# Thresholded attention with an ELU layer: scores that begin 64 columns further in their PSUM banks, and eight score products in another order

## The chip, the cores and the metric

The kernel runs on one core of one Trainium2 chip. The metric is device time in microseconds (us) of one execution; before the change the median of three runs is 1311.3 us (1310.9 to 1311.52).

## What is computed

Two blocks follow each other. For each of 8 sequences and 8 heads, with 576 tokens and 64 numbers per head, in float32:

```python
scores = (1/8) * q @ k.T                                  # 576 x 576 for each head
scores = where(scores >= max(scores) - tau, scores, -1e9)
attn   = exp(scores - max(scores)); attn /= sum(attn) + 1e-9
x      = attn @ v                                         # heads side by side: 4608 x 512
h      = x @ w_in                                         # 512 -> 2048
out    = where(h > 0, h, exp(min(h, 0)) - 1) @ w_out      # 2048 -> 512
```

## The kernel before

**Tiling.** Heads are handled in 32 pairs. The head dimension of 64 fills half of the 128 rows of TensorE, so that head 0 of a pair lies on rows 0 to 63 and head 1 on rows 64 to 127 (`r = slice(h * D, (h + 1) * D)`): products of the two heads use different halves of the array. The 576 queries of a pair are four tiles of 128 (`i` = 0 to 3) and a rest of 64 for both heads together (`i` = 4). P is 128, S 576, D 64, T 32, TAIL 64.

**The stage that matters here.** The first nine pairs run another scheme. From pair 9 on (`JOINED`), a loop over the pairs `pr` issues for each: `tail_step` (the scores of the 64 last queries, L672; the products with v of the pair two before, L677 and L685), then for `half` = 0 and 1 a `wide_step` (L1501), each followed by 14 quarters of the feed-forward block (L1238 is the product with w_in, L1378 that with w_out). There are 23 such pairs, and so 46 wide steps. Pairs alternate between two kinds of feed-forward work: after some, both halves are followed by L1238, after others by L1378.

**A wide step.** `wide_scores` computes scores of two query tiles (`s` = 0, 1) and two heads (`h` = 0, 1), four blocks of 128 x 576 numbers, into one PSUM tile of 128 x 2560, which is five banks of 512 columns. Block (h, s) begins at column (2h + (s xor h)) x 576, so that the order in the tile is (0,0), (0,1), (1,1), (1,0), and the last 256 columns are unused. A product must not cross a bank, so each block is cut in two where a bank ends: eight products, issued in an order written out by hand (L620). Each names the head `h`, the tile `s`, the first key column `c` and the number of columns `n`; its stationary operand is 128 queries of `qT`, its moving operand `n` keys of `kT`, and it appears twice in the profile, as two passes. After the eight products comes, on VectorE, a maximum of each block (L632), on GpSimd the bound (L638), on ScalarE the exponential (L642), and on VectorE the mask (L646).

**What waits for what.** `on_banks` (L586) makes dependencies by bank: a product waits for the ScalarE and VectorE instructions that touched its bank since the last product there, and a reader waits for all products into the banks it reads. In the product loop there is also a one-column ScalarE copy into `seen` (L628), which reads block (1,1) in bank 2 after its first piece: through it the last product of the step, also in bank 2, waits for that piece. In `tail_step` the products with v use banks 1 and 2 and are copied out by ScalarE (L695, L701); the tail's scores use banks 3 and 4 and are read by VectorE and ScalarE.

**Order.** Instructions of each engine run in the order in which they are issued. That order is fixed when the program is made: `on_pe` advances a planned TensorE clock by a planned cost (2.15 us for `wide_scores`), and `at` puts the other engines' work on an agenda by planned times, shifted by a table of corrections. The planned costs are numbers in the code, not measurements of a run.

Of the kernel before, what the change touches and what calls it, by code (L numbers as in the profile page):

```python
# [137 lines left out]
def kernel(  # L138
# [13 lines left out]
    B, H, S, D = q.shape  # L152
# [5 lines left out]
    T = 32  # L158
# [427 lines left out]
    def on_banks(made, ap):  # L586

        ins, needed, starts = made.ins, [], [ap.offset % (5 * 512)]
        for step, n in ap.ap[1:-1]:
            starts = [s + step * k for s in starts for k in range(n)]  # L590
        engine = str(ins.engine)
        for x in sorted({b for s in starts for b in range(s // 512, (s + ap.ap[-1][1] - 1) // 512 + 1)}):
            others = [i for e, i in accesses.setdefault(x, []) if e != engine]
            needed += others
            if others and engine == str(nc.tensor.engine):
                accesses[x] = []
            accesses[x].append((engine, ins))
        for other in needed:
            tc.add_manual_dep(ins, other.name,
                              mybir.DependencyInfo(mybir.DependencyClass.Sync, mybir.DependencyReason.DATA), reason="bank")  # L600
        for e in (nc.tensor, nc.scalar, nc.vector):
            if str(e.engine) != engine:
                tc.declare_no_dep(ins, group=str(e.engine), keep=needed, reason="other banks")
        tc.add_to_no_dep_group(engine, ins)

    def open_step(pr, i, w):
        st = open_steps[pr, i] = vectors(pr)
        st["w"] = w
        return st

    def wide_scores(pr, half):

        qT, kT, _ = pairs[pr]
        for s in range(2):
            i = 2 * half + s
            st = open_step(pr, i, turned_by[1 - s])
            for h in range(2):
                c = (2 * h + (s ^ h)) * S
                st["sc", h], st["e", h] = wide[0][:, c : c + S], st["w"][:, h * S : (h + 1) * S]
        for h, s, c, n in ((0, 0, 0, 512), (1, 1, 0, 384), (0, 0, 512, 64), (1, 1, 384, 192),  # L620
                           (1, 0, 0, 320), (0, 1, 0, 448), (1, 0, 320, 256), (0, 1, 448, 128)):
            i, r = 2 * half + s, slice(h * D, (h + 1) * D)
            k0 = c + (0 if h else TAIL)
            o = open_steps[pr, i]["sc", h][:, c : c + n]
            on_banks(nc.tensor.matmul(o, qT[r, i * P : (i + 1) * P], kT[r, k0 : k0 + n], start=True, stop=True,  # L625
                                      skip_group_check=True), o)
            if n == 384:
                on_banks(nc.scalar.copy(seen, o[:, :1]), o[:, :1])  # L628

    def wide_max(pr, i, h):  # L630
# [545 lines left out]
    with tc.manual_schedule():  # L1176
# [324 lines left out]
        def wide_step(pr, half):  # L1501
            t = clock[0]
            on_pe(2.15, lambda: wide_scores(pr, half))
            e = t + 2.15
            for s in range(2):
                i = 2 * half + s
                at(e + 1.55 + 1.5 * s, lambda i=i: wide_bounds(pr, i), f"bound{i}")
                for h in range(2):
                    k = 2 * s + (h ^ s)
                    at(e + 0.75 * k, lambda i=i, h=h: wide_max(pr, i, h), f"max{i}{h}")  # L1510
                    at(e + (1.6, 3.0, 4.7, 5.6)[k], lambda i=i, h=h: wide_exp(pr, i, h), f"exp{i}{h}")
                    at(e + (3.0, 4.3, 6.5, 6.9)[k], lambda i=i, h=h: wide_mask(pr, i, h), f"mask{i}{h}")
                finish_of(pr, i, e + (5.1, 7.8)[s], e + (8.4, 10.5)[s])
            if pr + 1 < NP:
                at(e + 5.2, lambda: (prep_k if half else prep_q)(pr + 1), f"prep{half}")
                if not half:
                    at(e + 6.1, lambda: scale_q(pr + 1), "qscale")
                if half:
                    at(e + 6.1, lambda: copy_k(pr + 1), "kcopy")
                    if pr + 2 < NP:  # L1520
                        at(e + 6.1, lambda: load(pr + 2, ("qm",), True), "loadq")
                elif pr > JOINED:
                    at(e + 6.1, lambda: load(pr + 1, ("km",), True), "loadk")
            extras(e + 0.3, e + 1.2, e + 4.2, e + 10.4, e + 12.0)
# [126 lines left out]
```

## Time and profile before

The profiled execution took 1310.99 us, of which the span of the core is 1309.2 us.

| what | value |
|---|---|
| median of three runs | 1311.3 us |
| profiled execution, its span | 1310.99 us, 1309.2 us |
| TensorE (PE) busy | 1294.1 us, 99% of the span |
| VectorE (DVE) busy | 1016.5 us, 78% |
| GpSimd (POOL) busy | 802.8 us, 61% |
| ScalarE (ACT) busy | 559.6 us, 43% |
| granted TensorE clock, mean of the span | 1.0 |
| first and last score product of a wide step (L625) | 292.1 us, 1062.0 us |

A profile row such as "PE f L1238 MATMUL" names the engine, the tile that is written, the line and the operation. PEld stands for loads of the stationary operand. In a row the shape "64*128 64x512" means 64 rows by 128 columns of the array, and 512 columns streamed on 64 partitions. Passes on TensorE are pipelined, so the recorded durations of neighbouring passes overlap, and what a pass occupies is the distance from its start to the next start. Idle time of an engine that does not set the end costs nothing.

### The profile page before, as it was taken

The numbers are of one execution on the slowest core, as the hardware profiler recorded it, in microseconds if no ns is written. First come the engines' busy times: TensorE is split into PE (matmuls) and PEld (weight loads), VectorE is DVE, ScalarE is ACT, GpSimd is POOL, SyncE is SP. The second block draws the span as 40 slices with busy tenths as digits, with TensorE's granted clock in tenths as the row PEclk, the third lists the DMA queues.
The fourth block names the chain that finished last, engine by engine and source line by source line (L and its number), as shares of the span: only waits on it lengthen the run. The fifth ranks groups of instructions, "written<-read, shape, count | busy, mean of one in ns | idle before, by whom it ended". The sixth has DMA issues, their size and how long they took to land.

```text
span 1309.2 us, 21968 instructions
## 1 busy us (share of the span) xinstructions
PE 1294.1 (99%) x6971; PEld 1007.7 (77%) x6971; DVE 1016.5 (78%) x2199; ACT 559.6 (43%) x1216; POOL 802.8 (61%) x1186
## 2 busy tenths in 40 slices
PE   9999999999999999999999999999999999999998
PEld 7667656556788887777777787777777888888887
DVE  6878886879888988898889979897989882545534
ACT  5677763225252535344444434352525260421320
POOL 4667875777466765766576747574858473624533
PEclk9999999999999999999999999999999999999999
DMA  6344655987888988898979888989899875221211
GB/s 138 77 106 125 177 111 140 258 229 219 222 233 237 258 227 251 220 268 209 245 211 264 231 234 225 258 235 240 229 253 256 221 215 173 92 73 60 93 61 33
DMA packets 323379, 248.94 MB, mean 190 GB/s; under 512 B 208832, under 2 KB 285120, under 8 KB 323264
## 3 DMA queue, kind: packets, MB, share of 16 engines
q1 hardware_dynamic: 321328, 247.06, 69.2%
q8 instruction: 55, 0.90, 0.3%
q10 hardware_dynamic: 1936, 0.48, 0.2%
q14 instruction: 60, 0.49, 0.1%
HBM read 162.40 MB, written 85.07 MB: 189 GB/s over the span
## 4 chain that ended last, share of the span: by engine, by line
PE 92%; DVE 4%; DMA 1%; issue 1%; POOL 1%; SPq 1%; ACT 0%; DVEq 0%; POOLq 0%; ACTq 0%
PE f L1378 29%; PE f L1238 29%; PE sc L625 8%; PE sc L685 7%; PE f L776 4%; PE rt L438 3%; PE sc L367 3%; PE f L736 3%; PE pv L578 2%; PE sc L677 1%; PE sc L672 1%; PE pv L573 1%; DVE w L428 1%; DMA there<-x 0%; POOL w L401 0%
## 5 line engine op out<-in xcount | busy, mean ns | idle before, releaser
L401 POOL TENSOR_SCALAR w<-w,rs 128x576 f32<-128x576 f32 x196 | 164.8, 848 | 80.7 <-DVE rs L435 65.5
L632 DVE TENSOR_REDUCE mx<-sc 128x1 f32<-128x576 f32 x207 | 148.2, 749 | 35.7 <-PE sc L625 33.0
L642 ACT ACTIVATE w<-sc,mx 128x576 f32<-128x576 f32 x115 | 83.0, 740 | 114.4 <-DVE mx L632 96.8
L1238 PE MATMUL f<-xt,sw 128*128 128x256 f32 x512 | 123.8, 384 | 0.8 <-ACT xt L695 0.5
L1238 PE MATMUL f<-xt,w_in_sb 128*128 128x256 f32 x512 | 122.4, 381 | 0.3 <-ACT w L1252 0.3
L638 POOL TENSOR_SCALAR th<-mx,ntau 128x2 f32<-128x2 f32 (+1 forms) x115 | 34.3, 298 | 141.2 <-DVE mx L632 141.2
L512 DVE STREAM_TRANSPOSE x<-w 128x512 f32<-128x512 f32 (+2 forms) x146 | 98.1, 706 | 13.5 <-POOL w L401 12.9
L1238 PEld LDWEIGHTS f<-xt,w_in_sb 128*128 128x128 f32 x512 | 96.1, 190 | 16.1 <-ACT w L1252 3.3
L1238 PEld LDWEIGHTS f<-xt,sw 128*128 128x128 f32 x512 | 93.7, 190 | 18.2 <-ACT xt L695 0.9
L625 PE MATMUL sc<-kT,qT 64*128 64x512 f32 (+4 forms) x736 | 107.5, 423 | 0.0
L1238 PE MATMUL f<-x,w_in_sb 128*128 128x256 f32 x448 | 106.1, 379 | 1.3 <-ACT g L1299 1.3
L625 PEld LDWEIGHTS sc<-kT,qT 64*128 64x128 f32 x736 | 80.8, 186 | 34.2 <-issue 16.8
L1378 PE MATMUL f<-w_out_sb,g 128*128 128x256 f32 x448 | 107.1, 382 | 0.0
L1378 PE MATMUL f<-w_out_sb,s 128*128 128x256 f32 x448 | 107.0, 382 | 0.0
L1378 PE MATMUL f<-t,s 128*128 128x256 f32 x448 | 105.8, 379 | 0.0
L1325 POOL TENSOR_TENSOR s<-g 128x256 f32<-128x256 f32 x104 | 80.3, 778 | 29.4 <-PE f L1378 20.1
L646 DVE SCALAR_TENSOR_TENSOR w<-sc,th,w 128x576 f32<-128x576 f32 x115 | 89.7, 810 | 10.3 <-ACT w L642 10.1
L1238 PEld LDWEIGHTS f<-x,w_in_sb 128*128 128x128 f32 x448 | 85.0, 190 | 13.3 <-ACT g L1299 1.7
L1378 PEld LDWEIGHTS f<-w_out_sb,g 128*128 128x128 f32 x448 | 84.1, 190 | 12.9 <-issue 0.7
L1378 PEld LDWEIGHTS f<-t,s 128*128 128x128 f32 x448 | 85.1, 190 | 11.6
L1378 PEld LDWEIGHTS f<-w_out_sb,s 128*128 128x128 f32 x448 | 84.2, 190 | 12.3
L401 POOL TENSOR_SCALAR e<-e,rs 128x576 f32<-128x576 f32 x92 | 68.5, 748 | 35.8 <-DVE rs L435 34.5
(189 smaller groups left out, 2853.7 us busy)
## 6 DMA issues: line engine op xcount, KB each, us to landing
there<-x SPq DMA_DIRECT2D x412, 144.0 KB, 3.5
wTb<-there SPq DMA_DIRECT2D x53, 576.0 KB, 6.3
wTa<-there SPq DMA_DIRECT2D x50, 576.0 KB, 5.0
sw<-win_sums SPq DMA_DIRECT2D x62, 384.0 KB, 4.3
t<-wout_sums SPq DMA_DIRECT2D x45, 512.0 KB, 5.4
qm<-in_q_dram SPq DMA_DIRECT2D x124, 72.0 KB, 4.5
vm<-in_v_dram SPq DMA_DIRECT2D x64, 128.0 KB, 3.4
wst<-in_moe_w_in_dram SPq DMA_DIRECT2D x16, 512.0 KB, 4.0
```

The costliest lines, as they stand in the source:

```text
L367: nc.tensor.matmul(scs[h][:, a, :HALF], qs[r], kT[r, k0 : k0 + HALF], start=True, stop=True)
L401: nc.gpsimd.tensor_scalar(wv, wv, st["rs"][:, h : h + 1], 1.0, ALU.mult, ALU.mult)
L512: nc.vector.transpose(x[:, :, c0 : c0 + nc_], src.rearrange("p (c g n) -> p g c n", c=nc_, n=T))
L625: on_banks(nc.tensor.matmul(o, qT[r, i * P : (i + 1) * P], kT[r, k0 : k0 + n], start=True, stop=True, skip_group_check=True), o)
L632: on_banks(nc.vector.tensor_reduce(st["mx"][:, h : h + 1], st["sc", h], axis=AX.XY if i == NC else AX.X, op=ALU.max, negate=True), st["sc" ...
L642: on_banks(nc.scalar.activation(st["e", h], st["sc", h], AF.Exp, bias=st["mx"][:, h : h + 1]), st["sc", h])
L646: on_banks(nc.vector.scalar_tensor_tensor(st["e", h], st["sc", h], st["th"][:, h : h + 1], st["e", h], ALU.is_ge, ALU.mult, accum_out=st[" ...
L685: on_banks(nc.tensor.matmul(o, vm[:, h, c], parts[part][:, g0:g1, h * (NC + 1) + c], start=False, stop=(c == NC - 1), skip_group_check=Tru ...
L776: nc.tensor.matmul(cur[c, i][:, :DM], hidden(c, ft % NU, 1)[:, 0, ft // NU, i], w_out_sb[:, ft], start=(ft == 0), stop=(ft == NFT - 1))
L1238: nc.tensor.matmul(loc["banks"][place], left[:, j], right[:, j], start=(begins and j == 0), stop=(j == 1), skip_group_check=True)
L1325: engine.tensor_tensor(o, x, y, op)
L1378: nc.tensor.matmul(place(m), lhs, rhs, start=(begins and v == 0), stop=(v == RU - 1), skip_group_check=True)
```

## The change

Every block of a wide step begins 64 columns (2 x T) further in the five banks. The bank ends therefore cut the blocks elsewhere: 448 + 128, 384 + 192, 320 + 256 and 256 + 320 columns instead of 512 + 64, 448 + 128, 384 + 192 and 320 + 256. No product has 64 columns any more. The eight products are issued in another order, and the condition that places the `seen` copy names the first piece of block (1,1) directly. Each block still lies in the same two banks as before.

```diff
             for h in range(2):
-                c = (2 * h + (s ^ h)) * S
+                c = 2 * T + (2 * h + (s ^ h)) * S
                 st["sc", h], st["e", h] = wide[0][:, c : c + S], st["w"][:, h * S : (h + 1) * S]
-        for h, s, c, n in ((0, 0, 0, 512), (1, 1, 0, 384), (0, 0, 512, 64), (1, 1, 384, 192),
-                           (1, 0, 0, 320), (0, 1, 0, 448), (1, 0, 320, 256), (0, 1, 448, 128)):
+        for h, s, c, n in ((0, 0, 0, 448), (1, 1, 0, 320), (1, 1, 320, 256), (0, 0, 448, 128),
+                           (1, 0, 0, 256), (0, 1, 0, 384), (1, 0, 256, 320), (0, 1, 384, 192)):
...
-            if n == 384:
+            if (h, s, c) == (1, 1, 0):
                 on_banks(nc.scalar.copy(seen, o[:, :1]), o[:, :1])
```

The order of instructions on VectorE, ScalarE, GpSimd and SyncE is the same in both programs; on TensorE only these eight products differ.

## The prediction

> **What bounds the kernel now.** I read the page first, then the busy time by stretch, because the change touches only the score products at L625, which run from 292 to 1062 us.
>
> ```profile
> span 1309.2 us, 21968 instructions
> PE 1294.1 (99%) x6971; PEld 1007.7 (77%) x6971; DVE 1016.5 (78%) x2199; ACT 559.6 (43%) x1216; POOL 802.8 (61%) x1186
> PE 92%; DVE 4%; DMA 1%; issue 1%; POOL 1%; SPq 1%; ACT 0%; DVEq 0%; POOLq 0%; ACTq 0%
> ```
>
> ```profile
> 292.00:340.00 48.00, 45.99 (x227) 35.49 (x226) 41.71 (x94) 23.25 (x51) 36.02 (x54) 1.00 0.78 207
> 340.00:1062.00 722.00, 722.00 (x4049) 576.50 (x4048) 625.84 (x1380) 309.37 (x682) 464.81 (x697) 1.00 0.88 238
> ```
>
> The columns are the stretch, its length, and busy time of PE, PEld, DVE, ACT and POOL. From 340 to 1062 us PE is busy for all of 722 us at the full granted clock, and the chain of waits for that stretch consists of PE lines alone. DVE is busy for 625.84 / 722 = 87%. So PE time taken out of a wide step should move the end, as long as the others can follow.
>
> Busy says nothing of stalls between passes, so I read the score products by shape.
>
> ```profile
> L625 PE MATMUL sc<-kT,qT 64*128 64x512 f32 x92 | 51.6, 641 | 0.0
> L625 PE MATMUL sc<-kT,qT 64*128 64x448 f32 x92 | 44.6, 565 | 0.0
> L625 PE MATMUL sc<-kT,qT 64*128 64x384 f32 x92 | 41.8, 534 | 0.0
> L625 PE MATMUL sc<-kT,qT 64*128 64x320 f32 x92 | 32.1, 429 | 0.0
> L625 PE MATMUL sc<-kT,qT 64*128 64x256 f32 x92 | 27.2, 376 | 0.0
> L625 PE MATMUL sc<-kT,qT 64*128 64x192 f32 x92 | 22.3, 323 | 0.0
> L625 PE MATMUL sc<-kT,qT 64*128 64x128 f32 x92 | 17.5, 270 | 0.0
> L625 PE MATMUL sc<-kT,qT 64*128 64x64 f32 x92 | 15.2, 245 | 0.0
> ```
>
> The last two fields are the union of busy time and the mean of one pass in ns. The last view is a stretch of PE in order of time: start, length, count.
>
> ```profile
> 713.73 1.89 PE L1238 MATMUL f<-xt,w_in_sb 128*128 128x256 f32 x8
> 715.46 1.89 PE L1238 MATMUL f<-x,w_in_sb 128*128 128x256 f32 x8
> 717.27 2.32 PE L625 MATMUL sc<-kT,qT 64*128 64x512 f32 x16
> 719.52 1.99 PE L1238 MATMUL f<-xt,sw 128*128 128x256 f32 x8
> ```
>
> A wide step occupies PE from 717.27 to 719.52, 2.25 us; 45 of the 46 take this time, and one (324.90 to 327.96) takes 3.06.
>
> **Where the 2.25 us go.** In the rows by shape, 128, 192, 256 and 320 columns lie on a line: (429 - 270) / 192 = 0.83 ns a column, plus 164 ns in which the end of a pass runs on beside the next. Eight passes of 256 columns take 715.46 - 713.73 = 1.73 us, 216 ns each, so a start costs some 3 ns above the columns. By the line, 512 and 384 columns should show 589 and 483 ns; they show 641 and 534, 52 and 51 more. These are the first pieces of the two halves of the array: on the first of two passes a weight load of about 104 ns lies open. The 64 columns should show 217 and show 245; the 448, which follow them in the same half, should show 536 and show 565. That is 2 x 28 + 2 x 29 = 114 ns. I read it so: a pass of 64 columns streams for 53 ns, the load for the pass behind it takes 104, and about 51 of each load lie open, twice. The 192, 256, 320 and 128 show nothing.
>
> The halves run beside each other. Each streams 1152 columns in two passes: 2 x 1152 x 0.83 = 1.91 us, 8 starts x 3 ns = 0.02, the first load 0.10: 2.04. The half of head 0 adds the 0.114: 2.15. The change-over to the next kind of product is 717.27 - 715.46 - 1.73 = 0.08. Sum 2.23 against 2.25 measured. So the half of head 0, with its 64 columns, ends the step, and the half of head 1 is done 0.1 us before it (in the trace its last pass starts 1.84 us into the step and streams 0.21; that of head 0 starts at 2.05 and streams 0.11).
>
> **The change part by part.**
>
> Removed: the 64 columns with their 0.114 us. Added: 128 columns in the middle of head 0's half. A pass of 128 streams for 106 ns against a load of 104, and the last product of before (128 columns) shows 270 ns, on the line; but there only its own second load is seen, and not one of a product behind it. I take 0.009 us for it, between 0 and 0.02. Both halves still stream 1152 columns. Gain per step 0.114 - 0.009 = 0.105 us; from 45 steps 4.7 us. In the long step the half of head 1 is held by a ScalarE copy until 0.95 us and ends last; nothing is gained or lost there.
>
> The queue order costs nothing if a piece's load is only held by the pieces ahead of it and by its own half. The trace shows that the halves pass each other:
>
> ```profile
> L625 PE MATMUL sc<-kT,qT 64*128 64x512 f32 x1 | 0.6, 589 | 0.0
> L625 PE MATMUL sc<-kT,qT 64*128 64x192 f32 x2 | 0.5, 322 | 0.0
> ```
>
> These are the passes in flight from 737.98 to 738.01 us: both passes of the fourth piece (192) and none of the third (64), which stands ahead of it but waits behind the 512 columns of its own half. By this, in the new order the pieces of head 1 start at 0, 0.65, 1.08 and 1.51 us, those of head 0 at 0, 0.86, 1.08 and 1.72, none late.
>
> Here a rule of the Trainium skill differs, "TensorE: Matmul & The Clock Gate", Part 3, The mechanism: matmuls start and end strictly in program order, and weight loads overlap running matmuls only when the row group differs. By the first half of it the old order would run as 1280 columns and the new one as 1152, and the gain would be 128 x 2 x 0.83 ns x 45 = 9.6 us; the rows just shown contradict it for this kernel. The second half speaks against the change, since pieces two and three now share a half; a row named with the rivals contradicts it too.
>
> The waits. Third in the queue is now a piece in bank 3; in first halves it waits for the mask of the tail scores (L646), which by the trace ends 1.39 us before the step in pairs of one kind and 0.25 us after its start in the others. Its load is due at about 0.54 (start 0.65 less a load), so 0.25 us of cover; if the mask came later than that, every 0.1 us would cost as much in 11 steps, and everything behind it on PE would wait too. The 128 columns in bank 1 wait for the copy L695, which ends 0.49 us into the step, and are due at 0.75. The `seen` copy now starts at 1.20 and ends at 1.36; it waits for both first pieces, of which the longer one shrinks from 512 to 448 columns, so I put it at 1.10 to 1.26; the last product's load is due at 1.39. All three cost nothing. The first maximum waits for the sixth product, which ends at 2.10 us; it should end at 1.88, so DVE may begin 0.2 us earlier where it is idle. Nothing on PE in this stage waits for that maximum directly.
>
> What gives some back:
>
> ```profile
> PEld sc L625 <- ACT xt L695: 5.1, 21, 0.2
> PEld f L1238 <- ACT w L1252: 2.3, 10, 0.3
> ```
>
> These are loads that waited between 340 and 1063 us (total, times, longest). The first is the copy just named and is covered. The second comes once in two pairs, 11 us after a second half: ScalarE stands behind DVE work which is busy from before the step, and some 0.1 us of each wait reaches PE. If PE comes 0.105 us earlier and that chain does not, 10 x 0.105 = 1.05 us are lost; if the chain moves along, nothing. I take the middle, 0.5. No other wait on PE is left in that stretch; what becomes late next is this one.
>
> Sum: 4.7 - 0.5 = 4.2 us. The profiled execution's 1310.99 becomes 1306.8; the median of the runs lies 0.3 above it, so 1311.3 becomes 1307.1.
>
> **The rivals.**
>
> No change that can be told (a measurement of this kernel can tell about 0.2%, 2.6 us): the open loads belong to the place in the queue and not to the 64 columns, so that the new 128 columns in the middle cost as much; or DVE, busy for 87%, keeps the pace and PE waits for what it saved. Against the first: 51 open of 104 is just what 53 ns of streaming leave. Against the second: PE waits for DVE's work only in those 10 places. Time 1309 to 1311.3.
>
> Slower: pieces two and three share a half, and the loads of both passes of the second one lie open, 2 x 104 = 0.208 us a step on the half that then ends last. Net 0.208 - 0.105 = 0.103 x 45 = 4.6 us, 1315.9. It decides from about 0.1 us open per step. Against it: in the old order 192 and 320 of head 1 are neighbours too, and the 320 show 429 ns, on the line. For it: only that no neighbours stood so early in the step.
>
> **How the numbers follow.** Forecast 0.83, no change 0.11, slower 0.06. The forecast's own range goes from 1305.4 (4.7 gained, and the ten waits of 0.1 gone as DVE starts earlier, with 0.2 for the scatter of the runs) to 1308.7, the bound of 0.2%. To leave out no more than 2 in 10, the range goes on through most of the no-change case, to 1310.6.
>
> **What would show it.** In the changed profile a wide step should last 2.14 to 2.15 us from its first pass to the next line. The row of 448 columns should lie some 52 ns above the line, that of 320 some 26 (one of its two pieces stands first in its half), and 128, 192, 256 and 384 on it. PE should still be busy through the stage, and the span of the 46 steps shorter by 4 to 5 us. The prediction is wrong if the 128 or the 384 show 25 ns or more above the line (the load stays open), if 256 does (the neighbours), if PE shows new waits for L646 at L625, or if L1252 holds PE for over 0.2 us each time.

## The result and the profile after

The changed kernel takes 1307.2 us in the median of 7 runs (1306.34 to 1307.65) against 1311.52 us for the kernel before, run beside it. The ratio is 0.9965, with a 95% interval of 0.9956 to 0.9974: 3.4 to 5.8 us less. The profiled execution has a span of 1305.3 us, 3.9 less than before.

The page of the changed kernel, first line, busy time of the engines and the chain that ended last:

```profile
span 1305.3 us, 21968 instructions
PE 1289.7 (99%) x6971; PEld 1008.4 (77%) x6971; DVE 1015.5 (78%) x2199; ACT 559.7 (43%) x1216; POOL 802.5 (61%) x1186
PE 92%; DVE 4%; issue 1%; POOL 1%; DMA 1%; ACT 1%; SPq 1%; DVEq 0%; POOLq 0%; ACTq 0%
```

TensorE lost 4.4 us of busy time; the other engines did the same work. Busy time by stretch, with the columns as in the prediction:

```profile
340.00:1058.00 718.00, 717.63 (x4049) 576.98 (x4049) 625.03 (x1381) 309.35 (x682) 464.61 (x697) 1.00 0.88 240
```

The stretch ends where the last score product starts, at 1058.1 us instead of 1062.0, and PE is still busy through it, but for 0.37 us. The score products by shape (union of busy time, mean ns of a pass):

```profile
L625 PE MATMUL sc<-kT,qT 64*128 64x320 f32 x184 | 69.0, 455 | 0.0
L625 PE MATMUL sc<-kT,qT 64*128 64x256 f32 x184 | 47.1, 376 | 0.0
L625 PE MATMUL sc<-kT,qT 64*128 64x448 f32 x92 | 46.7, 588 | 0.0
L625 PE MATMUL sc<-kT,qT 64*128 64x384 f32 x92 | 37.1, 484 | 0.0
L625 PE MATMUL sc<-kT,qT 64*128 64x192 f32 x92 | 22.3, 323 | 0.0
L625 PE MATMUL sc<-kT,qT 64*128 64x128 f32 x92 | 17.6, 272 | 0.0
```

The line through the rows of before (164 ns + 0.83 ns a column) gives 270, 323, 376, 483, 430 and 536 for 128, 192, 256, 384, 320 and 448 columns. Only 448 (52 above) and 320 (25 above, half of its passes) are off it: the first pieces of the two halves. The stretch that answers to the one of before, PE in order of time:

```profile
713.32 1.89 PE L1238 MATMUL f<-x,w_in_sb 128*128 128x256 f32 x8
715.13 2.21 PE L625 MATMUL sc<-kT,qT 64*128 64x448 f32 x16
717.28 1.99 PE L1238 MATMUL f<-xt,sw 128*128 128x256 f32 x8
```

From 715.13 to 717.28 a wide step now takes 2.14 us by the trace (2.15 in these rounded rows), where it took 2.25. So do 45 of the 46 steps; the long one stays at 3.06.

Three of the waits on the way to TensorE between 340 and 1060 us in the changed kernel (total, times, longest): first two kinds of weight loads, then a product.

```profile
PEld f L1238 <- ACT w L1252: 2.1, 9, 0.3
PEld f L1238 <- DMA there<-x: 0.9, 4, 0.2
PE f L1238 <- DMA sw<-win_sums: 0.4, 1, 0.4
```

The loads that waited for the copy L695 (5.1 us in 21 times before) are gone, the waits for L1252 are as they were, and one product waits 0.4 us for a transfer that it did not wait for before. The short waits for another transfer (there<-x) are new, but they reach no product: by the trace, the times between one wide step and the next are within 0.04 us of before everywhere except at that one product.

To see where the time went, I took from each trace the distance from the first pass of a wide step to the first pass of the next line, for all 46 steps, and the rest. The table has the changed kernel and the experiments told below. Differences to the profiled execution of before, in us:

| kernel | before the first step | in 46 steps | between them | after the last | span |
|---|---|---|---|---|---|
| changed | +0.44 | -4.84 | +0.52 | +0.03 | -3.85 |
| changed, second profile | +1.20 | -4.84 | +1.85 | -0.02 | -1.80 |
| width alone | +0.26 | -4.73 | +0.43 | -0.06 | -4.11 |
| order alone | +0.63 | 0.00 | +0.38 | 0.00 | +1.01 |
| 32 columns further | +1.39 | -2.51 | -0.02 | -0.05 | -1.20 |
| 64 columns last | +1.14 | -2.40 | +3.42 | +0.01 | +2.17 |
| 128 columns last | +0.99 | -4.82 | +3.69 | -0.03 | -0.16 |
| 64 + 64 | +0.36 | +5.13 | -1.21 | -0.07 | +4.21 |
| 128 columns further | +0.34 | -4.84 | -0.39 | -0.03 | -4.92 |

The time before the first step, which none of these edits touches, moves by up to 1.4 us from execution to execution, and the time between the steps differs by 1.3 us between the two profiles of the changed kernel; the steps themselves are the same to 2 ns each in those two profiles. So a theory of the step is tested on the second column, and the others say what came of it.

### The profile page after: what moved, and what is told of

Same layout as the page of the kernel before. It is cut to its first block, busy times and chain, and to the rows that moved or that the text cites. A ratio compares the mean times of both kernels' runs of the same rounds, so it can differ in the third digit from the quotient of the medians.

```text
span 1305.3 us, 21968 instructions
## 1 busy us (share of the span) xinstructions
PE 1289.7 (99%) x6971; PEld 1008.4 (77%) x6971; DVE 1015.5 (78%) x2199; ACT 559.7 (43%) x1216; POOL 802.5 (61%) x1186
## 4 chain that ended last, share of the span: by engine, by line
PE 92%; DVE 4%; issue 1%; POOL 1%; DMA 1%; ACT 1%; SPq 1%; DVEq 0%; POOLq 0%; ACTq 0%
PE f L1378 29%; PE f L1238 28%; PE sc L625 7%; PE sc L685 7%; PE f L776 4%; PE rt L438 4%; PE sc L367 3%; PE f L736 3%; PE pv L578 2%; PE sc L677 1%; PE sc L672 1%; DVE w L428 1%; DVE mx L405 1%; PE pv L573 1%; POOL w L401 0%
## 5 line engine op out<-in xcount | busy, mean ns | idle before, releaser
L642 ACT ACTIVATE w<-sc,mx 128x576 f32<-128x576 f32 x115 | 83.0, 740 | 115.6 <-DVE mx L632 98.0
L1238 PE MATMUL f<-xt,sw 128*128 128x256 f32 x512 | 123.9, 384 | 1.2 <-ACT xt L695 0.5
L1238 PE MATMUL f<-xt,w_in_sb 128*128 128x256 f32 x512 | 122.3, 381 | 0.3 <-ACT w L1252 0.3
L1238 PEld LDWEIGHTS f<-xt,sw 128*128 128x128 f32 x512 | 93.7, 190 | 21.3 <-issue 5.5
L1238 PEld LDWEIGHTS f<-xt,w_in_sb 128*128 128x128 f32 x512 | 96.2, 190 | 16.0 <-ACT w L1252 3.0
L1238 PE MATMUL f<-x,w_in_sb 128*128 128x256 f32 x448 | 106.1, 379 | 1.3 <-ACT g L1299 1.3
L625 PE MATMUL sc<-kT,qT 64*128 64x448 f32 (+4 forms) x736 | 102.6, 416 | 0.0
L625 PEld LDWEIGHTS sc<-kT,qT 64*128 64x128 f32 x736 | 81.0, 186 | 24.3 <-issue 16.8
L646 DVE SCALAR_TENSOR_TENSOR w<-sc,th,w 128x576 f32<-128x576 f32 x115 | 89.7, 809 | 10.2 <-ACT w L642 10.1
L1238 PEld LDWEIGHTS f<-x,w_in_sb 128*128 128x128 f32 x448 | 85.0, 190 | 13.3 <-ACT g L1299 1.7
```

Source lines behind the costliest of these rows:

```text
L642: on_banks(nc.scalar.activation(st["e", h], st["sc", h], AF.Exp, bias=st["mx"][:, h : h + 1]), st["sc", h])
L646: on_banks(nc.vector.scalar_tensor_tensor(st["e", h], st["sc", h], st["th"][:, h : h + 1], st["e", h], ALU.is_ge, ALU.mult, accum_out=st[" ...
L1238: nc.tensor.matmul(loc["banks"][place], left[:, j], right[:, j], start=(begins and j == 0), stop=(j == 1), skip_group_check=True)
```

## The experiments

Theory: a pass of 64 columns streams for a shorter time than the weight load behind it takes, and what is left of the load lies open (width). The load records of the kernel before look like it: in a step of its trace the loads for the second pass of 64 columns and for the two passes of 448 behind it start at 0.965, 1.075 and 1.186 us, 0.11 us apart, where a pass of 64 streams for 0.053. Rival: the gain comes from the new order of the queue (order). The first four kernels ran beside a kernel before of 1311.96 us (27 runs), the other four beside 1312.01 (18 runs).

**Width alone.** The new columns, the old alternation of halves.

```diff
-        for h, s, c, n in ((0, 0, 0, 448), (1, 1, 0, 320), (1, 1, 320, 256), (0, 0, 448, 128),
-                           (1, 0, 0, 256), (0, 1, 0, 384), (1, 0, 256, 320), (0, 1, 384, 192)):
+        for h, s, c, n in ((0, 0, 0, 448), (1, 1, 0, 320), (0, 0, 448, 128), (1, 1, 320, 256),
+                           (1, 0, 0, 256), (0, 1, 0, 384), (1, 0, 256, 320), (0, 1, 384, 192)):
```

> The blocks begin 64 columns further as in the change, but the eight products keep the old alternation of halves (first pieces, second pieces, ...). Width theory (a pass of 64 columns is shorter than the weight load behind it): no 64 columns are left, so a wide step lasts 2.14 us as in the changed kernel, and the median lies about 4.3 us under that of before. Order theory (the gain comes from the new order of the queue): the step stays at 2.25 us and the median at that of before.

Measured: 1307.45 us, ratio 0.9967 (0.9954 to 0.9979). The first line is its waits between 340 and 1060 us, the other two a step in order of time:

```profile
PEld sc L625 <- ACT xt L695: 5.1, 21, 0.2
```

```profile
427.99 2.21 PE L625 MATMUL sc<-kT,qT 64*128 64x448 f32 x16
430.14 1.99 PE L1238 MATMUL f<-xt,sw 128*128 128x256 f32 x8
```

The whole gain is there without the new order. The order is worth 0.1 us over all steps: here the third product stands in bank 1 and waits for L695, the fourth waits behind it, and some 20 steps last 2.145 instead of 2.141 us.

**Order alone.** The old columns, the new alternation.

```diff
+                c = (2 * h + (s ^ h)) * S
...
+        for h, s, c, n in ((0, 0, 0, 512), (1, 1, 0, 384), (1, 1, 384, 192), (0, 0, 512, 64),
+                           (1, 0, 0, 320), (0, 1, 0, 448), (1, 0, 320, 256), (0, 1, 448, 128)):
```

> The blocks begin at the old columns, so 512 + 64 and the other old widths stay, but the products come in the new alternation of halves. Width theory: step 2.25 us, the row of 64 columns near 245 ns and that of 448 near 565, median that of before (within 1 us). Order theory: step 2.14 us and 4.3 us less.

Measured: 1311.79 us, ratio 1.0001 (0.9993 to 1.001). Two of its rows by shape, the 64 columns and the 448 behind them:

```profile
L625 PE MATMUL sc<-kT,qT 64*128 64x448 f32 x92 | 44.6, 565 | 0.0
L625 PE MATMUL sc<-kT,qT 64*128 64x64 f32 x92 | 15.2, 245 | 0.0
```

Same rows, same step (2.25 us), same time as before. The order theory falls.

**32 columns further.** The smallest piece has 96 columns.

```diff
+                c = 32 + (2 * h + (s ^ h)) * S
...
+        for h, s, c, n in ((0, 0, 0, 480), (1, 1, 0, 352), (1, 1, 352, 224), (0, 0, 480, 96),
+                           (1, 0, 0, 288), (0, 1, 0, 416), (1, 0, 288, 288), (0, 1, 416, 160)):
```

> The blocks begin 32 columns further than before: the smallest piece has 96 columns instead of 64 or 128, in the new order. Width theory: a pass of 96 columns streams for 80 ns, a load takes 104 to 107, so 24 to 27 ns lie open twice: step 2.14 + 0.05 = 2.19 us, rows of 96 and of 416 columns (which follow them) each 12 to 14 ns above the line (164 ns + 0.83 ns a column), median about 2 us above that of the changed kernel. A theory in which 64 columns are a special case (a fixed floor under which a pass can't go): 96 columns cost nothing, step 2.14 us.

Measured: 1309.71 us, ratio 0.9983 (0.9974 to 0.9993), steps of 2.193 us. Two rows by shape, and a step:

```profile
L625 PE MATMUL sc<-kT,qT 64*128 64x416 f32 x92 | 40.9, 524 | 0.0
L625 PE MATMUL sc<-kT,qT 64*128 64x96 f32 x92 | 16.4, 258 | 0.0
```

```profile
429.48 2.26 PE L625 MATMUL sc<-kT,qT 64*128 64x480 f32 x16
431.68 1.56 PE L1238 MATMUL f<-xt,sw 128*128 128x256 f32 x6
```

96 columns should show 244 and show 258; 416 should show 509 and show 524. That is 2 x 14 + 2 x 15 = 58 ns, about 29 for each of the two open loads, where 64 columns left 57: the open part shrinks by 28 ns for 32 columns, about what they stream longer (27). The steps say the same: 52 ns above those of the change, 26 a load, against 107 ns and 54 a load with 64 columns. So 64 columns are no special case; what lies open is some 107 ns (53 streamed and 54 open, or 80 and 26) less the streaming time. The first load of a step, which has nothing ahead of it, is open for 52 x 2 = 104 ns. That fits the length of a load; the runs do not separate it from some other least distance of 107 ns between two passes of one half, which would give the same sums.

**64 columns last.** Old widths, but in head 0's half the order 512, 448, 128, 64.

```diff
+        for h, s, c, n in ((0, 0, 0, 512), (1, 1, 0, 384), (1, 1, 384, 192), (0, 1, 0, 448),
+                           (1, 0, 0, 320), (0, 1, 448, 128), (1, 0, 320, 256), (0, 0, 512, 64)):
```

> Old columns and widths, but the 64 columns come last in their half (512, 448, 128, 64), with nothing of the step behind them. Width theory with two open loads (that of the second pass of 64 and that of the piece behind it): only the first is left, step 2.14 + 0.05 = 2.19 to 2.20 us, the row of 64 near 245 ns, that of 448 on the line (536). Theory that a piece of 64 columns costs 0.11 us wherever it stands: step 2.25 us. The first maximum on VectorE now waits for the last product, some 0.1 us later than before the change; that costs nothing on TensorE by either theory.

Measured: steps of 2.195 us, as expected, but 1312.93 us, ratio 1.0007 (0.9998 to 1.0016). By shape:

```profile
L625 PE MATMUL sc<-kT,qT 64*128 64x448 f32 x92 | 42.0, 537 | 0.0
L625 PE MATMUL sc<-kT,qT 64*128 64x64 f32 x92 | 15.2, 245 | 0.0
```

The 448 are back on the line, 64 keeps its own open load: one load is open instead of two, 2.4 us less in the steps. But 3.4 us came back between them, 5 x 0.52 in every second pair of the kind with L1238 and 0.05 to 0.16 in a dozen other places, 0.8 in all. My sentence that a later first maximum costs nothing was wrong. In order of time around one of the five, first before, then this kernel:

```profile
433.23 0.68 DVE L904 TENSOR_TENSOR xt<-xt 128x512 f32<-128x512 f32 x1
433.32 1.18 POOL L1257 TENSOR_TENSOR u<-u,w 128x256 f32<-128x256 f32 x1 [0.54 <-ACT u L1252]
```

```profile
434.37 0.72 POOL L1257 TENSOR_TENSOR u<-u,w 128x256 f32<-128x256 f32 x1 [0.32 <-ACT u L1252]
434.50 1.14 DVE L904 TENSOR_TENSOR xt<-xt 128x512 f32<-128x512 f32 x1
```

Two additions, one on VectorE and one on GpSimd, meet; whichever starts second takes some 0.46 us longer. Before, GpSimd was second by 0.09 us, and TensorE did not wait for it. Here VectorE began its first maximum 2.30 us into the step instead of 2.14, and L904 comes second, by 0.13 us. A product of TensorE needs its result: it starts at 435.79, just behind the end of L904 at 435.64. (The profile puts this wait down to ScalarE's L642, whose count moved last; the ScalarE copy that the product needs had ended at 435.05. In the kernel before, the same product starts at 434.29, while L642 still runs until 434.65: it does not need L642.)

**128 columns last.** To part the late maximum from the 64 columns: the widths of the change, with the first block's second piece at the end.

```diff
+        for h, s, c, n in ((0, 0, 0, 448), (1, 1, 0, 320), (1, 1, 320, 256), (0, 1, 0, 384),
+                           (1, 0, 0, 256), (0, 1, 384, 192), (1, 0, 256, 320), (0, 0, 448, 128)):
```

> Columns and widths of the change, but in the half of head 0 the 128 columns come last (448, 384, 192, 128), so that the first maximum on VectorE (L632) waits for the last product, as in the run with 64 columns last, and starts near 2.25 us into the step instead of 1.92. Theory that the late first maximum ate that run's gain (VectorE's L904 then starts behind GpSimd's L1257, takes 1.14 us instead of 0.68 and holds TensorE for 0.52 us in five places): step 2.14 us, but L904 at 1.14 again and some 3 us given back between the steps; median about 1310 to 1311. Theory that a pass of 64 columns at the end of the step did it: L904 at 0.68, nothing given back, median 1307.4.

Measured: 1310.63 us, ratio 0.9988 (0.9979 to 0.9997). From its order of time:

```profile
433.86 0.72 POOL L1257 TENSOR_TENSOR u<-u,w 128x256 f32<-128x256 f32 x1 [0.30 <-ACT u L1252]
434.01 1.12 DVE L904 TENSOR_TENSOR xt<-xt 128x512 f32<-128x512 f32 x1
```

The steps gain 4.82 us as in the change, and 3.69 come back, 5 x 0.52 of it in the same five places. The first maximum starts 2.26 us into the step, against 1.92 in the change. So the late first maximum does it, not the 64 columns, as far as the five places go; the other 1.1 us lie in a dozen places, 0.05 to 0.17 each. In most of them loads of L1238 now wait for VectorE's L1260 too (8 waits, 1.5 us in all, which is more than reaches the products); that is not traced further. So the place of the first block's second piece, fourth in the queue, matters to the change after all, though not through TensorE.

**64 + 64.** The 128 columns of the change cut in two.

```diff
-        for h, s, c, n in ((0, 0, 0, 448), (1, 1, 0, 320), (1, 1, 320, 256), (0, 0, 448, 128),
-                           (1, 0, 0, 256), (0, 1, 0, 384), (1, 0, 256, 320), (0, 1, 384, 192)):
+        for h, s, c, n in ((0, 0, 0, 448), (1, 1, 0, 320), (1, 1, 320, 256), (0, 0, 448, 64), (0, 0, 512, 64),
+                           (1, 0, 0, 256), (0, 1, 0, 384), (1, 0, 256, 320), (0, 1, 384, 192)):
```

> The changed kernel with its 128 columns cut into 64 + 64, nine products a step: the suspected cost doubled against the kernel of before. Width theory: four loads lie behind passes of 64 columns, 4 x 51 to 57 ns = 0.20 to 0.23 us, step 2.14 + 0.20 to 0.23 = 2.34 to 2.37 us, row of 64 near 245 to 270 ns, the median some 9 to 10 us above the changed kernel if the other engines follow. Theory that one short piece is covered by the other half anyway and only its place mattered: 2.14 to 2.25 us.

Measured: 1315.89 us, ratio 1.0029 (1.0019 to 1.0039). A step in order of time:

```profile
429.32 2.43 PE L625 MATMUL sc<-kT,qT 64*128 64x448 f32 x18
431.69 1.56 PE L1238 MATMUL f<-xt,sw 128*128 128x256 f32 x6
```

A step is 2.36 us, 0.222 longer than in the change: 55 ns for each of four open loads. The steps add 9.97 us to those of the change; the median rises 8.4 above that of the changed kernel beside it, because the time between the steps shrinks: 1.2 us of it against before, most of which is 0.09 us at each place where L1252 was waited for and TensorE now comes later.

**128 columns further.** The smallest piece has 192 columns.

```diff
+                c = 128 + (2 * h + (s ^ h)) * S
...
+        for h, s, c, n in ((0, 0, 0, 384), (1, 1, 0, 256), (1, 1, 256, 320), (0, 0, 384, 192),
+                           (1, 0, 0, 192), (0, 1, 0, 320), (1, 0, 192, 384), (0, 1, 320, 256)):
```

> The blocks begin 128 columns further than before: the smallest piece has 192 columns, order of halves as in the change. Width theory: a load is covered by any pass of 128 columns or more, so the step is 2.13 to 2.14 us and the median that of the changed kernel within 1 us. Theory that the piece of 128 columns still leaves something open: the step falls below 2.12 us and the median below 1306.5.

Measured: 1306.88 us (1305.84 to 1306.97), ratio 0.9956 (0.9944 to 0.9968); steps of 2.14 us, to a few ns those of the change:

```profile
427.94 2.21 PE L625 MATMUL sc<-kT,qT 64*128 64x384 f32 x16
430.08 2.00 PE L1238 MATMUL f<-xt,sw 128*128 128x256 f32 x8
```

The step alone does not show that 128 columns cover the load, because the half of head 1 now ends it: by the trace, the last passes of the two halves (start plus columns x 0.83 ns) end 2.046 us (head 0) and 2.048 us (head 1) into a step of the change, and 2.040 and 2.047 in a step here. So head 0 won some 6 ns from 192 columns instead of 128, and they are hidden behind head 1. In the change the passes behind the two of 128 columns start 0.109 and 0.111 us after them, 3 and 5 ns more than 128 columns stream. The load is covered to within a few ns, and since both halves end together, nothing more is to be had from width. This version lies 0.6 us under the changed kernel of the same session, but their runs overlap, and the steps are the same; it is not shown to be faster.

**The changed kernel again.**

> The changed kernel once more, for a second profile beside that of the prediction. If the wait of 0.4 us for a transfer of sums of w_in near 994 us (sw from win_sums) belongs to the change (TensorE arrives earlier there than the transfer), it stands here again; if it is scatter between executions, it is absent or at another place. The step is 2.14 us either way.

Measured: 1307.5 us (1306.26 to 1309.18), ratio 0.9964 (0.9952 to 0.9977).

```profile
PE f L1238 <- ACT w L642: 1.4, 2, 0.7
```

The wait in the half that begins near 994 us is here again and costs 0.8 us, and others stand in the halves that begin near 445 (0.77) and 582 (0.24); this execution took 1309.18, the longest of its five. The view names ScalarE's L642, but by the trace the product starts 0.13 to 0.14 us after the last packet of the transfer of sw has landed, in all three places and in the first profile too: it is the transfer. With the order alone, where the steps last as before, there is one of 0.45 us at 445; 32 and 128 columns further have none of that size. So the waits come and go, at few places, and do not need the change; whether it makes the one at 994 more likely (three of the five profiles with steps of 2.14 us show it; with 128 columns further and with 128 columns last it is absent) stays open.

## Why the prediction was right

**The step.** The row-by-row working held. The excess of 64 and 448 columns was taken for 0.114 us, less 0.009 left open at 128; measured are 0.107 a step (2.248 to 2.141), 4.84 us in all, against 4.7 forecast. The open load was read as 51 ns; it is 53 to 55 by the steps and 57 by the rows. 45 steps gained and the long one did not (3.06 and 3.06), as said.

**The waits of the new order** cost nothing: no wait for L646 appears at L625, and the `seen` copy starts 1.10 us into the step as forecast. The first maximum starts 1.93 us into the step (430.11 in the step at 428.18), 0.2 earlier, as forecast.

**What is given back** is the term that failed. I took 0.5 us off at L1252, as the middle of 0 and 1.05. The waits there stayed as they were (9 of 2.1 us in total, after 10 of 2.3; in the tenth place stands the wait for the transfer). By the trace the product that waits starts 301 to 317 ns after the one ahead of it, before the change 305 to 309, where 216 is usual (leaving out one place where two waits follow each other): some 90 ns each time, as before. The chain of VectorE and ScalarE moved along with the step, most likely because its first maximum came 0.2 us earlier. The other runs speak for it: with 128 columns further, where that maximum starts at 1.81 us and the step is as long, the distances are 272 to 291 ns, and with a late maximum new waits arise. In place of the 0.5, the profiled execution lost 0.52 at the transfer and 0.44 before the first step, both of a kind that comes and goes. That the total fits so well, 4.3 us against 4.2, owes something to this.

**The rivals.** Order of the queue: excluded by the two crossed runs. VectorE keeping the pace: in the change it did not, yet with 64 or 128 columns last it took back 2.6 us by one operation that came second (of 3.4 and 3.7 lost between the steps), which is the rival's mechanism in a place I had not priced. Neighbours in one half with their loads open: the 256 columns, second of the neighbours, show 376 ns, on the line. So the rule cited for it does not hold here, and neither does the strict order of starts: in the run with width alone the fourth product starts at 0.65 us, the third at 0.86. On TensorE, then, the order of issue is not always the order of starts.

## What to carry to other kernels

Look at small matmul pieces by shape: where the mean of one shape, and of the shape behind it, lies above the line through the others, a weight load is likely open, and each pass of the piece should stream for at least as long as a load takes (here some 107 ns, which is 128 columns). Where two halves of the array run beside each other, only the half that ends last counts: in the long step, which head 1 ends, the same change of widths gained nothing. And choose the order of pieces not only for TensorE: let the piece that the first reader waits for come early, since 0.2 us there decided who came second at a meeting of VectorE and GpSimd, and that was worth 2.6 of the 4.8 us.

## What the runs showed of the hardware that was not expected

VectorE's addition L904 takes 0.68 us beside GpSimd's L1257 when it starts 0.09 us before it and 1.14 us when it starts 0.13 after it; GpSimd's takes 1.18 and 0.72 in turn. The Trainium skill describes this ("SBUF — State Buffer", Who interferes with whom): a VectorE instruction with two inputs in SBUF contends with a GpSimd instruction that reads SBUF, the lock between them is exclusive, and the order of issue decides who waits. The lengths here agree with it, and the runs add that a shift of 0.22 us between the two was enough to change the winner.
